# An FFT filter and an MLP on one core: the transform's steps are given out ahead of the inverse's step in the loop over products

## The chip, the core and the metric

The kernel runs on one core of one Trainium2 chip. The metric is the device time of one execution in microseconds (us). A core has five engines that work side by side, each through its own list of instructions in order: TensorE (PE, matrix products, with its weight loads shown as PEld), VectorE (DVE), ScalarE (ACT), GpSimd (POOL) and SyncE (SP), which here does nothing but issue transfers between the device memory and the core. An instruction waits until the data that it reads is there and the buffer that it writes is free.

## What is computed

The reference, cut to what matters. Input x has 8 batches of 3136 positions by 256 channels.

```python
X = np.fft.rfft(x, axis=1)
Y = X * (filt_r + 1j * filt_i)
x = np.fft.irfft(Y, n=3136, axis=1)          # the filtered sequence

X = np.fft.fft(np.fft.fft(x, axis=1), axis=2)
u = x + np.real(X)
un = (u - mean(u)) / np.sqrt(var(u) + 1e-06) # over the channels
out = u + np.maximum(un @ w_ch1, 0.0) @ w_ch2   # 256 -> 1024 -> 256
```

## The kernel before

The two transforms along the sequence cancel in part, so one pass forward and one inverse pass do the work, each as two stages of small matrix products.

*Transform of a batch b* (`there`, 63 steps, `STEPS`). Seven loads bring the batch (`x_b_0` to `x_b_6`, 512 KB each, issued by SP at L399). The largest value of each load is taken, on DVE by a reduction (`mx_b`, L283) or, for batches 1 and 2, on ACT by squares (`xsq_b`, L405). From these a scale is made, which one small product on PE spreads over the partitions (`pb_x`, L276). Fourteen first-stage products follow (`s1_b_0` to `s1_b_13`, L429 for batches 1 and 2, L443 for the others); ACT and DVE write each out (`ast`, L431 and L432) and SP stores it in device memory (`d1<-ast`, L433 or L447). SP reads it back in another order (`at_b_0` to `at_b_6`, L468); the second stage multiplies it (`s<-at`, L493 and L494), the filter is applied on DVE and POOL, a transposing transfer gives `z_b_0` to `z_b_6` (L528), and the inverse's first stage multiplies these (`i<-z`, L563 to L565). Its results are stored (`d2<-bt`, L572).

*Second inverse stage of a batch* (`back`, 17 steps, `BACK`). SP loads `b2_b_0` to `b2_b_6` (L606), PE multiplies (`y_b_0` to `y_b_13`, L629), ACT writes out (`ys`, L639), SP stores (`dy<-ys`, L612).

*Groups of 512 positions* (49 of them, about six to a batch). Group g is fetched from `dy` (`y_g`, L700) and `prepare` makes its input in small pieces: two sets of products on PE (`mix_g`, L713), additions on DVE (L723), the statistics (L782, L783) and the factor `sb_g` (L789 to L798), the normalised value on ACT (`un`, L805), its high and low 16-bit parts on ACT and POOL (`u16`, L808 and L810), and two transposing transfers on SP (`ut_g`, L819).

*Products.* Each group has eight: `h_g_0` to `h_g_7` (L843, six matmuls each), which ACT and DVE turn into `h16` (L852, L853), and for each the part of the second matrix that it feeds (`acc_g_0` and `acc_g_1`, L872, twelve matmuls), two products later (`LAG`). DVE adds the finished `acc` to `y_g` (L881), and SP stores it (`out<-y`, L884).

*The order of the work.* The loop at L1062 goes over all 394 products. In each turn it gives out the first product, a piece of `prepare` of a later group, the second product of two turns before, then at most one step of the inverse's second stage (`give`, L1074), then as many steps of the transform as its progress asks for (`advance`, L1075). `give` stops while the transform of its batch has not been given out to its last but one step (L991); `advance` stops at the start of a batch while the batch before the last has not had its inverse begun (L982). Both only hand work to a scheduler, which keeps its own account of when each engine would be free and ready, and which prefers what was given out earlier where several instructions could go. So the order in which the steps are given out is a rank, and the list of each engine can differ from it. Buffers come from pools with few places (four banks of results for the transform and the small products, two for `h`, two for `acc`, seven places that `x`, `at` and `z` share).

Of the kernel before, what the change touches and what calls it, by code (L numbers as in the profile page):

```python
# [38 lines left out]
STEPS = FIRST + PAUSE + 7 * 5  # L39
WAIT = 2  # L40
BACK = 1 + WAIT + 14
EARLY = 0.6
RISE = 28
# [150 lines left out]
def program(tc, a, NB):  # L194
    nc = tc.nc
    with ExitStack() as ctx:
        _program(ctx, tc, nc, a, NB)


def _program(ctx, tc, nc, a, NB):  # L200
# [491 lines left out]
    def fetch(g):  # L692
        y = ys_of[g] = mp.tile([128, 2, 2, 256], F32, tag="y", name=f"y_{g}", bufs=4)
        for t, (g0, g1) in enumerate(groups[g]):
            q = g0
            while q < g1:
                b = q // NS
                e = min(g1, (b + 1) * NS)
                with after(("un", 0)) if g == 2 else after(("out", g - 4)):
                    marks["y", g] = nc.sync.dma_start(  # L700
                        y[q - g0 : e - g0, t], dys[b][:, q - b * NS : e - b * NS].rearrange("k s c -> s k c")
                    ).ins
                q = e
# [125 lines left out]
    def first_product(g, f):  # L829
        y, ut = ready[g]  # L830
        m = groups[g][0][1] - groups[g][0][0]
        nt = 2 * sum(g1 - g0 for g0, g1 in groups[g])
        utv = ut[:, : len(groups[g])].rearrange("p t (k d l) q -> p t k d l q", k=2, d=2)
        p = ps_h.tile([128, 512], F32, tag="psh", name=f"h_{g}_{f}")
        even = nt == 2 * m * len(groups[g])
        runs = [(slice(0, len(groups[g])), 0, nt, m)] if even else [
            (slice(t, t + 1), 256 * t, 2 * (g1 - g0), g1 - g0) for t, (g0, g1) in enumerate(groups[g])
        ]
        for ts, c0, n, m in runs:
            i = 0  # L840
            for d in range(2):
                for hw, hx in ((0, 0), (0, 1), (1, 0)):
                    marks["pe"] = nc.tensor.matmul(  # L843
                        p[:, c0 : c0 + n].rearrange("p (t k q) -> p t k q", k=2, q=m),
                        w1s[:, d, hw, 128 * f : 128 * f + 128],
                        utv[:, ts, :, d, hx, :m],
                        start=i == 0,
                        stop=i == 5,
                    ).ins
                    i += 1  # L850
        h = mp.tile([128, 2, 512], F16, tag="h", name=f"h16_{g}_{f}", bufs=4)
        marks["relu"] = nc.scalar.activation(h[:, 0, :nt], p[:, :nt], AF.Relu).ins  # L852
        marks["h"] = nc.vector.scalar_tensor_tensor(  # L853
            h[:, 1, :nt], p[:, :nt], 0.0, h[:, 0, :nt], op0=ALU.max, op1=ALU.subtract
        ).ins
        hs[g, f] = h

    def second_product(g, f):
        tiles = groups[g]
        y = ready[g][0]  # L860
        h = hs.pop((g, f))
        if f == 0:
            accs[g] = [
                ps_o.tile([128, 2, 256], F32, tag="pso", name=f"acc_{g}_{t}") for t in range(len(tiles))
            ]
        c0 = 0
        for t, (g0, g1) in enumerate(tiles):
            m = g1 - g0
            acc = accs[g][t]
            for k in range(2):  # L870
                for i, (hh, hw) in enumerate(((0, 0), (0, 1), (1, 0))):
                    nc.tensor.matmul(  # L872
                        acc[:m, k],
                        h[:, hh, c0 : c0 + m],
                        w2s[:, f, hw],
                        start=f == 0 and k == 0 and i == 0,
                        stop=f == 7 and k == 1 and i == 2,
                    )
                c0 += m
            if f == 7:  # L880
                nc.vector.scalar_tensor_tensor(  # L881
                    y[:m, t], acc[:m], beta[:m], y[:m, t], op0=ALU.mult, op1=ALU.add
                )
                marks["sp"] = marks["out", g] = nc.sync.dma_start(a["out"][:, g0:g1].rearrange("k s c -> s k c"), y[:m, t]).ins  # L884
# [93 lines left out]
    def advance(n):  # L978

        while done[0] < min(n, NB * STEPS):  # L980
            b, s = divmod(done[0], STEPS)
            if s == 0 and come[0] < BACK * (b - 1) + 1:  # L982
                return
            if s in folds and b * NS + folds[s] - RING > mixed[0]:
                return
            next(forth)
            done[0] += 1

    def give(n):

        while come[0] < min(n, NB * BACK) and done[0] >= STEPS * (come[0] // BACK + 1) - 1:  # L991
            next(home)
            come[0] += 1
# [3 lines left out]
    def need(slot):  # L997

        return BACK * (slot // NS) + 1 + WAIT + 2 + 2 * (slot % NS // 224)

    def soon(slot):

        return max(need(slot), BACK * ((slot + LOADED) // NS) + 1 + WAIT)

    def bring(slot):
        advance(STEPS * (slot // NS + 1) - 1)
        give(need(slot))
        assert come[0] >= need(slot)
# [52 lines left out]
    per = NS // 32  # L1061
    for q in range(8 * ng + LAG):  # L1062
        g, f = divmod(q, 8)
        if g < ng:
            first_product(g, f)
        if f == 8 - AHEAD:
            for _ in work:
                pass
            if g + 2 < ng:
                work = prepare(g + 2)  # L1070
        next(work, None)
        if q >= LAG:
            second_product(*divmod(q - LAG, 8))
        give(min(come[0] + 1, soon(32 * q + SOON)))  # L1074
        advance(int(STEPS * (1 + min((q + 1) / RISE, (q + 1) / per + EARLY))))  # L1075
        for ahead in [2] * (q == 0) + [g + 3] * (f == 6):
            if ahead < ng:
                bring(groups[ahead][-1][1] - 1)
                fetch(ahead)
# [59 lines left out]
```

## Time and profile before

| | |
|---|---|
| time, median of 3 runs | 1475.76 us (1474.89 to 1478.65) |
| the profiled execution, its own time | 1477.43 us |
| its span, first to last instruction | 1475.5 us |
| PE busy | 1421.5 us, 96% of the span |
| DVE, ACT, POOL busy | 72%, 52%, 36% |
| mean granted TensorE clock | 0.992 of full speed |
| moved by transfers | 280.55 MB, 190 GB/s over the span |

The profile gives, for one execution, the busy time of each engine, the idle time ahead of each instruction with the event that ended it, and the clock that TensorE was granted. Levels of that clock are 2.4 GHz (1.00) and 1.2 GHz (0.50). Idle time of an engine is dear only where what is late next hangs on it.

### The profile page before, as it was taken

What the parts mean: (1) busy time and instruction counts of PE and PEld (TensorE: products, weight loads), DVE (VectorE), ACT (ScalarE), POOL (GpSimd) and SP (SyncE); (2) the same over time, 40 slices, a digit from 0 to 9 for tenths busy, and PEclk for the clock granted to TensorE, in tenths of its full rate; (3) what the DMA queues carried; (4) which work ended last, traced back from release to release, by engine and by line L of the source; (5) the groups of instructions that cost most, each with busy time, mean ns of one, the idle gap of its engine ahead of it and who ended that gap; (6) DMA issues with size and microseconds to landing.
All of it is one profiled execution on the core that took longest, in us unless ns stands there. A gap on an engine that the chain in (4) does not pass through costs nothing.

```text
span 1475.5 us, 30603 instructions
## 1 busy us (share of the span) xinstructions
PE 1421.5 (96%) x11517; PEld 937.5 (64%) x11517; DVE 1069.5 (72%) x2341; ACT 767.4 (52%) x1420; POOL 532.6 (36%) x674
## 2 busy tenths in 40 slices
PE   7897999989999999999999999999999999999998
PEld 3644577546666676667766667666766667666666
DVE  6887677378878876977768876887868786545552
ACT  4766455555556454555447464565446555344341
POOL 4840186028510771038401672028400574010110
PEclk9999999999999999999999999999999999999999
DMA  9956778789976988589775987679684997553320
GB/s 334 325 171 181 199 174 172 251 216 235 226 206 167 203 203 238 148 218 232 164 241 165 234 192 208 183 204 246 153 242 126 220 217 161 142 139 96 86 58 29
DMA packets 445331, 280.55 MB, mean 190 GB/s; under 512 B 218944, under 2 KB 410752, under 8 KB 445184
## 3 DMA queue, kind: packets, MB, share of 16 engines
q1 hardware_dynamic: 445184, 278.61, 72.6%
q8 instruction: 90, 1.47, 0.4%
q14 instruction: 57, 0.47, 0.1%
HBM read 124.88 MB, written 102.79 MB: 154 GB/s over the span
## 4 chain that ended last, share of the span: by engine, by line
PE 67%; DMA 12%; DVE 7%; issue 4%; POOL 4%; ACT 3%; SPq 2%; DVEq 0%; ACTq 0%; POOLq 0%
PE h L843 26%; PE acc L872 25%; PE s L443 3%; DMA x<-x 3%; PE y L629 3%; PE mix L713 2%; DMA at<-d 2%; DMA z<-y 2%; PE s L429 1%; DVE y L723 1%; PE i L563 1%; PE s L493 1%; PE i L565 1%; PE i L564 1%; PE s L494 1%
## 5 line engine op out<-in xcount | busy, mean ns | idle before, releaser
L872 PE MATMUL acc<-w2s,h 128*128 128x256 f16 x4704 | 596.8, 273 | 4.4 <-DVE y L881 2.3
L843 PE MATMUL h<-ut,w1s 128*128 128x512 f16 x2352 | 586.1, 382 | 11.0 <-DVE h L853 4.8
L872 PEld LDWEIGHTS <-h 128*128 128x128 f16 x4704 | 455.9, 98 | 154.8 <-issue 21.5
L852 ACT ACTIVATE h<-h 128x512 f16<-128x512 f32 x392 | 233.1, 595 | 388.1 <-PE h L843 381.2
L853 DVE SCALAR_TENSOR_TENSOR h<-h,h 128x512 f16<-128x512 f32 x392 | 267.9, 685 | 212.5 <-ACT h L852 211.3
L843 PEld LDWEIGHTS <-w1s 128*128 128x128 f16 x2352 | 222.4, 98 | 223.6 <-issue 31.4
L810 POOL TENSOR_TENSOR u<-un,u 128x512 f16<-128x512 f32 x94 | 107.8, 1163 | 678.6 <-ACT u L808 636.7
L723 DVE SCALAR_TENSOR_TENSOR y<-mix,alpha,y 128x508 f32<-128x508 f32 (+1 forms) x368 | 156.1, 476 | 6.7 <-PE mix L713 3.8
L511 POOL TENSOR_TENSOR yt<-yt,t 128x224 f32<-128x224 f32 x112 | 76.5, 683 | 142.2 <-DVE t L507 72.5
L805 ACT ACTIVATE un<-y,sb 128x256 f32<-128x256 f32 x196 | 101.9, 590 | 38.0 <-DVE sb L798 33.9
L517 POOL TENSOR_TENSOR y<-yt,y 128x448 f16<-128x448 f32 x105 | 108.0, 1032 | 18.1 <-ACT y L516 17.9
L571 DVE TENSOR_TENSOR bt<-i,bt 112x512 f16<-112x512 f32 x112 | 76.0, 685 | 48.5 <-ACT bt L570 44.9
L639 ACT ACTIVATE ys<-y,alpha 128x512 f32<-128x512 f32 x112 | 75.9, 685 | 60.6 <-PE y L629 59.1
L570 ACT CAST bt<-i 112x512 f16<-112x512 f32 x112 | 64.5, 584 | 56.9 <-PE i L565 51.7
L881 DVE SCALAR_TENSOR_TENSOR y<-acc,beta,y 128x512 f32<-128x512 f32 x98 | 71.2, 744 | 30.8 <-PE acc L872 30.6
L503 DVE SCALAR_TENSOR_TENSOR yt<-s,pF,ft 128x448 f32<-128x448 f32 x112 | 75.4, 675 | 23.1 <-PE s L494 18.3
L516 ACT CAST y<-yt 128x448 f16<-128x448 f32 x112 | 62.8, 564 | 36.9 <-POOL yt L512 33.0
L556 POOL TENSOR_TENSOR eo<-ef,eo 128x448 f16<-128x448 f32 (+6 forms) x62 | 60.8, 983 | 44.2 <-ACT eo L555 42.7
L507 DVE SCALAR_TENSOR_TENSOR t<-s,pF,ft 128x448 f32<-128x448 f32 x112 | 75.6, 675 | 0.4 <-POOL yt L512 0.3
L535 POOL TENSOR_TENSOR ef<-yt 128x224 f32<-128x224 f32 x112 | 74.1, 679 | 1.6
L512 POOL TENSOR_TENSOR yt<-yt,t 128x224 f32<-128x224 f32 x112 | 73.7, 660 | 0.0
L629 PE MATMUL y<-b,i 112*64 112x512 f16 (+1 forms) x480 | 70.2, 375 | 3.0 <-DMA b<-d 1.3
(131 smaller groups left out, 1656.7 us busy)
## 6 DMA issues: line engine op xcount, KB each, us to landing
x<-x SPq DMA_DIRECT2D x56, 512.0 KB
at<-d SPq DMA_DIRECT2D x56, 512.0 KB
b<-d SPq DMA_DIRECT2D x56, 512.0 KB
d<-ast SPq DMA_DIRECT2D x112, 224.0 KB
d<-bt SPq DMA_DIRECT2D x112, 224.0 KB
out<-y SPq DMA_DIRECT2D x98, 256.0 KB
y<-dy SPq DMA_DIRECT2D x92, 256.0 KB
dy<-ys SPq DMA_DIRECT2D x208, 112.0 KB
```

What stands on the lines that cost most here:

```text
L511: nc.gpsimd.tensor_tensor(yh[:, 0], yh[:, 0], t2v[:, 1], op=ALU.subtract)
L517: last = half(b, hf == 1).tensor_tensor(ylo, ytv, yhi, op=ALU.subtract)
L571: marks["low"] = nc.vector.tensor_tensor(bt[:, :, 1], p, bt[:, :, 0], op=ALU.subtract).ins
L629: marks["i2"] = nc.tensor.matmul(p[64 * h : 64 * h + 64, js], i2[:, t, h, i], bt[:, o + js.start : o + js.stop, h], start=i == 0, stop=i == 1,
L639: nc.scalar.activation(ys[:, o : o + 2], p, AF.Copy, scale=al[:, 2:3])
L723: nc.vector.scalar_tensor_tensor(out, p, al, y, op0=ALU.mult, op1=ALU.add)
L805: nc.scalar.activation(un[:m, k], y[:m, t, k], AF.Identity, bias=sb[:m, i, 1:2], scale=sb[:m, i, 3:4])
L810: marks["u16", g] = low.tensor_tensor(u16[:m, :, :, 1], unv, u16[:m, :, :, 0], op=ALU.subtract).ins
L843: marks["pe"] = nc.tensor.matmul(p[:, c0 : c0 + n].rearrange("p (t k q) -> p t k q", k=2, q=m), w1s[:, d, hw, 128 * f : 128 * f + 128], ut ...
L852: marks["relu"] = nc.scalar.activation(h[:, 0, :nt], p[:, :nt], AF.Relu).ins
L853: marks["h"] = nc.vector.scalar_tensor_tensor(h[:, 1, :nt], p[:, :nt], 0.0, h[:, 0, :nt], op0=ALU.max, op1=ALU.subtract).ins
L872: nc.tensor.matmul(acc[:m, k], h[:, hh, c0 : c0 + m], w2s[:, f, hw], start=f == 0 and k == 0 and i == 0, stop=f == 7 and k == 1 and i == 2,)
```

## The change

Two lines of the loop over products change places. What each step does is the same, and no instruction is added or left out.

```diff
         if q >= LAG:
             second_product(*divmod(q - LAG, 8))
+        advance(int(STEPS * (1 + min((q + 1) / RISE, (q + 1) / per + EARLY))))
         give(min(come[0] + 1, soon(32 * q + SOON)))
-        advance(int(STEPS * (1 + min((q + 1) / RISE, (q + 1) / per + EARLY))))
```

Within a turn the transform's steps now rank ahead of the inverse's step. Each transform step stays in its turn. The first inverse step of batches 1 to 6, which had to wait for the transform steps of the turn before, is given out one turn earlier (batch 1 in turn 27 instead of 28). The scheduler makes other lists from this: 8891 of PE's 22910 rows, 795 of DVE's 2343, 549 of ACT's 1396, 215 of POOL's 679 and 406 of SP's 1070 stand at another place; what lies ahead of the loop is the same but for one small product (`y_0_10`, now inside the loop), and from about 1260 us on the lists are the same again.

**Place one, between batches 1 and 2 (around 260 to 317 us).** SP's list before, from the last but one load of batch 2 on; `dy_1`, `b2_1` belong to batch 1's second inverse stage, `out<-y_3` and `y_6` to groups (the trailing numbers are the program's own):

```order
L399 DMA x_2_5_3269<-x 128x1024
L606 DMA b2_1_1_3346<-d2_1_128 128x8x256
L884 DMA out<-y_3_1936 128x2x256
L612 DMA dy_1_3261<-ys_1_0_3348 28x256 x2
L612 DMA dy_1_3261<-ys_1_0_3348 28x4x256
L612 DMA dy_1_3261<-ys_1_0_3348 28x3x256
L612 DMA dy_1_3261<-ys_1_0_3348 28x4x256
L612 DMA dy_1_3261<-ys_1_0_3348 28x3x256
L606 DMA b2_1_2_3404<-d2_1_128 128x8x256
L399 DMA x_2_6_3270<-x 128x1024
```

and now:

```order
L399 DMA x_2_5_3269<-x 128x1024
L606 DMA b2_1_1_3346<-d2_1_128 128x8x256
L399 DMA x_2_6_3270<-x 128x1024
L884 DMA out<-y_3_1936 128x2x256
L612 DMA dy_1_3231<-ys_1_0_3348 28x256 x2
```

The last load of batch 2, `x_2_6`, has moved ahead of an output store, six stores and a load. DVE's list at the same place before, where `y_6` is group 6's additions, `ast_2` the write-out of batch 2's first stage and `h16_5` the products of group 5:

```order
L432 SCALAR_TENSOR_TENSOR ast_2_1_3516<-s1_2_1_3514,sx_2_3461,ast_2_1_3516 112x2x256
L853 SCALAR_TENSOR_TENSOR h16_5_4_4046<-h_5_4_4039,h16_5_4_4046 128x512
L432 SCALAR_TENSOR_TENSOR ast_2_2_3522<-s1_2_2_3520,sx_2_3461,ast_2_2_3522 112x2x256
L853 SCALAR_TENSOR_TENSOR h16_5_5_4101<-h_5_5_4094,h16_5_5_4101 128x512
L723 SCALAR_TENSOR_TENSOR y_6_3371<-mix_6_3536,al_6_0_3650,y_6_3371 128x4x127
```

and now:

```order
L432 SCALAR_TENSOR_TENSOR ast_2_1_3507<-s1_2_1_3505,sx_2_3451,ast_2_1_3507 112x2x256
L432 SCALAR_TENSOR_TENSOR ast_2_2_3513<-s1_2_2_3511,sx_2_3451,ast_2_2_3513 112x2x256
L723 SCALAR_TENSOR_TENSOR y_6_3371<-mix_6_3536,al_6_0_3650,y_6_3371 128x4x127
L723 SCALAR_TENSOR_TENSOR y_6_3371<-mix_6_3536,al_6_0_3650,y_6_3371 128x2x127 x2
L723 SCALAR_TENSOR_TENSOR y_6_3371<-mix_6_3536,al_6_0_3650,y_6_3371 128x4
L723 SCALAR_TENSOR_TENSOR y_6_3371<-mix_6_3536,alpha_1_2157,y_6_3371 128x4x127
L853 SCALAR_TENSOR_TENSOR h16_5_3_3987<-h_5_3_3980,h16_5_3_3987 128x512
```

Group 6's additions have moved ahead of group 5's `h16_5_3`, `h16_5_4` and `h16_5_5`. On PE the two sets of `mix_6` stand earlier by so many matmuls that lie between; worked out from the lengths of these, the first by 5.65 us of products and the second by 6.9 us, while `h_5_3` to `h_5_7` and the last `acc_5` stand later.

**Place two, between batches 6 and 7 (around 1095 us).** SP's list before:

```order
L399 DMA x_7_4_15077<-x 128x1024
L399 DMA x_7_5_15078<-x 128x1024
L606 DMA b2_6_2_15237<-d2_0_126 128x8x256
L399 DMA x_7_6_15079<-x 128x1024
L700 DMA y_36_15249<-dy_6_15005 64x2x256
```

and now:

```order
L399 DMA x_7_4_15077<-x 128x1024
L399 DMA x_7_5_15078<-x 128x1024
L399 DMA x_7_6_15079<-x 128x1024
L606 DMA b2_6_2_15240<-d2_0_126 128x8x256
L700 DMA y_36_15249<-dy_6_14976 64x2x256
```

The load `x_7_6` and the load `b2_6_2` have changed places.

**Place three, between batches 4 and 5 (around 754 to 768 us).** DVE's list before, where `mx_5` are the reductions over batch 5's loads and `h16_21` the products of group 21:

```order
L283 TENSOR_REDUCE mx_5_10337<-x_5_0_10330 112x1
L853 SCALAR_TENSOR_TENSOR h16_21_4_10384<-h_21_4_10377,h16_21_4_10384 128x512
L723 SCALAR_TENSOR_TENSOR y_23_10177<-mix_23_10287,alpha_3_6234,y_23_10177 128x4x127
L283 TENSOR_REDUCE mx_5_10337<-x_5_1_10331 112x1
L723 SCALAR_TENSOR_TENSOR y_23_10177<-mix_23_10287,alpha_3_6234,y_23_10177 128x2x127 x2
```

and now:

```order
L283 TENSOR_REDUCE mx_5_10337<-x_5_0_10330 112x1
L283 TENSOR_REDUCE mx_5_10337<-x_5_1_10331 112x1
L853 SCALAR_TENSOR_TENSOR h16_21_4_10384<-h_21_4_10377,h16_21_4_10384 128x512
L723 SCALAR_TENSOR_TENSOR y_23_10177<-mix_23_10299,alpha_3_6225,y_23_10177 128x4x127
L283 TENSOR_REDUCE mx_5_10337<-x_5_2_10332 112x1
```

One reduction has moved ahead of `h16_21_4`, and in the rows that follow one more each ahead of `h16_21_5`, `h16_21_6` and `h16_21_7`.

## Rows read from the trace of the kernel before

**Rows 1.** The page's table of engines: busy time, share of the span, instructions.

```profile
PE 1421.5 (96%) x11517; PEld 937.5 (64%) x11517; DVE 1069.5 (72%) x2341; ACT 767.4 (52%) x1420; POOL 532.6 (36%) x674
```

**Rows 2.** Stretches of 60 us: length, then the busy time of PE, PEld, DVE, ACT and POOL with their instructions, the granted clock, the busy share of the transfer engines, GB/s; the last row is the sum over 24 such stretches.

```profile
0.00:60.00 60.00, 51.63 (x432) 28.32 (x433) 43.81 (x82) 31.81 (x55) 35.44 (x54) 1.00 0.97 339
60.00:120.00 60.00, 51.38 (x376) 28.34 (x375) 50.03 (x101) 40.48 (x73) 27.84 (x31) 0.97 0.71 225
...
300.00:360.00 60.00, 55.05 (x500) 34.52 (x498) 47.20 (x109) 32.30 (x62) 35.42 (x48) 0.94 0.93 215
360.00:420.00 60.00, 57.87 (x481) 39.36 (x478) 46.15 (x88) 30.89 (x60) 27.41 (x34) 1.00 0.92 232
...
1260.00:1320.00 60.00, 60.00 (x440) 38.37 (x438) 32.59 (x89) 26.38 (x50) 6.67 (x6) 1.00 0.50 122
...
sum 1440.00, PE 1390.41 PEld 916.09 DVE 1059.14 ACT 760.82 POOL 532.61; mean PE 57.93 PEld 38.17 DVE 44.13 ACT 31.70 POOL 22.19
```

**Rows 3.** What PE waited for over the whole span: in total, times, longest, in us.

```profile
PE s L493 <- DMA at<-d: 10.5, 8, 3.0
PE pb_w L276 <- DVE lines_w L274: 5.2, 2, 4.8
PE h L843 <- DVE h L853: 4.8, 6, 1.4
PE i L563 <- DMA z<-y: 4.7, 5, 1.8
PE h L843 <- DMA dy<-ys: 4.7, 1, 4.7
...
PE acc L872 <- DVE y L881: 2.3, 1, 2.3
```

**Rows 4.** PE's instructions in order of time, from several short stretches: start, length, what; in brackets the idle time just before and what ended it.

```profile
181.59 0.20 PE L493 MATMUL s<-s,at 112*128 112x56 f16 x1 [1.87 <-DMA at<-d]
...
205.90 0.29 PE L563 MATMUL i<-z,i 112*112 112x256 f16 x1 [1.57 <-DMA z<-y]
...
379.86 1.47 PE L843 MATMUL h<-ut,w1s 128*128 128x512 f16 x6 [1.44 <-DMA ut<-u]
...
765.07 1.46 PE L843 MATMUL h<-ut,w1s 128*128 128x512 f16 x6 [1.35 <-DVE h L853]
...
985.76 0.20 PE L493 MATMUL s<-s,at 112*128 112x56 f16 x1 [2.14 <-DMA at<-d]
...
1106.88 1.14 PE L872 MATMUL acc<-w2s,h 128*128 128x256 f16 x8 [2.34 <-DVE y L881]
```

**Rows 5.** PE in order of time between batches 1 and 2, with the same columns: the product that waits for the scale, the two sets of `mix_6` and the first products of group 6.

```profile
276.39 1.46 PE L843 MATMUL h<-ut,w1s 128*128 128x512 f16 x6
...
281.49 0.21 PE L276 MATMUL pb_x<-lines_x,still 112*128 112x112 bf16 x1
...
289.41 0.56 PE L713 MATMUL mix<-mix,eo 128*128 128x129 f16 x8
...
291.89 0.56 PE L713 MATMUL mix<-mix,eo 128*128 128x129 f16 x8
...
317.02 3.57 PE L843 MATMUL h<-ut,w1s 128*128 128x512 f16 x8 [4.65 <-DMA dy<-ys]
```

**Rows 6.** SP's issues between batches 1 and 2, in order of time: an output store, a load of the inverse, the last load of batch 2, and the second transposing transfer of group 6.

```profile
260.76 5.67 SPq L884 DMA_DIRECT2D out<-y  x1
...
271.97 0.38 SPq L399 DMA_DIRECT2D x<-x  x1
...
312.47 1.70 SPq L819 DMA_TRANSPOSE ut<-u  x1
```

**Rows 7.** The chain of waits at the same place (start, length, what): the load `x_2_5`.

```profile
259.52 10.21 DMA x<-x
```

**Rows 8.** ACT in order of time at the same place: the square of the last load, `x_2_6`.

```profile
277.05 1.06 ACT L405 ACTIVATE xsq<-x 112x1024 bf16<-112x1024 f32 x1 [2.44 <-DMA x<-x]
```

**Rows 9.** Short stretches, with the columns of rows 2: two of heavy transfer at place one, the stretch of the low clock there, and the same at place two.

```profile
255.00:265.00 10.00, 10.00 (x74) 6.34 (x72) 1.93 (x6) 4.02 (x8) 0.00 (x0) 1.00 0.99 314
265.00:275.00 10.00, 8.55 (x59) 4.96 (x58) 2.77 (x4) 8.30 (x16) 0.00 (x0) 1.00 0.90 299
...
1100.00:1105.00 5.00, 4.14 (x25) 2.25 (x24) 2.07 (x5) 1.14 (x3) 0.00 (x0) 1.00 1.08 317
...
315.80:322.60 6.80, 5.58 (x15) 2.13 (x16) 3.07 (x15) 1.05 (x3) 0.00 (x0) 0.50 0.97 272
1107.70:1111.10 3.40, 3.40 (x12) 1.46 (x11) 1.63 (x6) 1.65 (x4) 0.00 (x0) 0.50 0.45 154
```

**Rows 10.** DVE in order of time at place two: the last two reductions over batch 7's loads, with the idle time before each.

```profile
1101.09 1.22 DVE L283 TENSOR_REDUCE mx<-x 112x1 f32<-112x1024 f32 x1 [1.39 <-DMA x<-x]
...
1104.88 1.22 DVE L283 TENSOR_REDUCE mx<-x 112x1 f32<-112x1024 f32 x1 [1.85 <-DMA x<-x]
```

**Rows 11.** SP's issues at place two: the two loads that change places.

```profile
1095.37 0.38 SPq L606 DMA_DIRECT2D b<-d  x1
1095.79 1.14 SPq L399 DMA_DIRECT2D x<-x  x1
```

**Rows 12.** DVE in order of time at place three: the first reduction over batch 5's loads and what follows it.

```profile
753.72 1.22 DVE L283 TENSOR_REDUCE mx<-x 112x1 f32<-112x1024 f32 x1 [2.47 <-DMA x<-x]
754.86 0.68 DVE L853 SCALAR_TENSOR_TENSOR h<-h,h 128x512 f16<-128x512 f32 x1
```

## The prediction

> **What bounds the kernel now.** I read the page's table of engines first. PE is busy for 1421.5 of 1475.5 us [rows 1], so the kernel is bound by PE's products, and since the change adds and drops none, the only time that it can win or lose is PE's idle time and the time that PE spends at the low clock. The stretches of 60 us say where idle time is: PE is busy 1390.4 of the first 1440 us, and 17.0 of the missing 49.6 us lie in the first 120 us (8.4 and 8.6), which the change leaves as they are. From 1260 us on PE is never idle [rows 2]. So some 32.6 us between 120 and 1260 us are all the idle time there is to win.
>
> The list of PE's waits says what ended it: reads of the transform's stage 1 (10.5 us in 8 waits), `h16` from DVE (4.8 in 6), `z` (4.7 in 5), one wait of 4.7 us at the first product of a group, one of 2.3 for an addition on DVE, and one of 4.8 at the scale of the weights ahead of the loop [rows 3]. All but the last are places where an instruction of the transform, the inverse or a group's preparation came late for PE's next row, and such places depend on the order in the lists. The two largest are in PE's own rows: 4.65 us ahead of the first product of group 6 (317.02) and 2.34 us ahead of group 34's second product (1106.88) [rows 4, 5]. The clock adds to both: from 315.8 to 322.6 and from 1107.7 to 1111.1 us the granted clock was 0.50, that is 1.2 GHz, after PE had stood idle, and PE was busy 5.58 and 3.40 us of these [rows 9]. At 2.4 GHz this work takes half, so the low clock cost 2.8 and 1.7 us.
>
> **The change, part by part.** No instruction comes or goes, so every edit is a move, and I price what each does to these waits.
>
> *Place one, group 6.* The wait named as `dy<-ys` at 317.02 is really for `ut_6`, whose second transposing transfer SP issued at 312.47 and was done issuing at 314.17 [rows 6]. Ahead of it lies the chain mix, additions, statistics, normalised value, `u16`. Before, the two sets of `mix_6` ran at 289.41 and 291.89 [rows 5]. By the order they now stand 5.65 and 6.9 us of products earlier, and DVE's list has the additions ahead of three `h16_5` rows. From the second set to the wait's end is a chain that needs no other late work, so `ut_6` comes about 6 us earlier and 4.65 are needed: the wait goes, and the low clock with it, -4.65 and -2.8. What is late next is the scale of batch 2. `pb_x` now stands where PE comes at about 276.6 (behind the product that starts at 276.39), and it ran at 281.49, 4.4 us after the square of `x_2_6` began at 277.05, which had waited for the load [rows 5, 8]. That load was issued at 271.97, held behind an output store that kept SP for 5.67 us from 260.76 [rows 6]. It now goes ahead of that store, so 11 us sooner, but into full transfer engines (busy 0.99 and 0.90) [rows 9]. The load ahead of it landed at 269.73 (259.52 + 10.21) [rows 7]. Two loads of 512 KB at 314 GB/s [rows 9], 3.3 us, bring `x_2_6` to 273.1 and `pb_x` to 277.5: a new wait of +0.9. Bounds: 0 if it lands at 272, +4.9 if it lands no sooner than before. I take +0.9, from the rates. Place one: -6.55.
>
> *Place two, batch 7's last load.* DVE works through its list in order: the reduction at 1104.88 had waited 1.85 us for `x_7_6`, the addition that frees PE's bank stood behind it, and PE waited 2.34 us [rows 4, 10]. SP now issues `x_7_6` ahead of `b2_6_2` instead of after it (1095.37 and 1095.79 [rows 11]). The reduction over the load before, which also waited, began at 1101.09, so the two landed 3.79 us apart with `b2_6_2` between them: 1.05 MB in that time is 277 GB/s, close to the 317 of that stretch [rows 9, 10]. So these transfers were served about in the order of issue, and the swap is worth half of the 3.79, 1.9, plus the issue slot of 0.4. I take -2.0 of the 2.34, and the low clock goes, -1.7. Bounds: 0 and -4.0. Place two: -3.7. The Trainium skill (DMA: Bandwidth & Descriptors, "Queues, rings and completion order") says that each transfer engine takes one issuer's descriptors in ring order, with which these rows agree, but also that a later transfer may complete before an earlier one. If the two loads simply shared the engines, the swap would give the issue slot alone, 0.4 us, the low clock would stay, and the sum would come out 3.3 us higher.
>
> *Place three, DVE at batch 5.* Four reductions move ahead of `h16_21_4` to `h16_21_7`. The next instruction starts 1.14 us after a reduction does (753.72 to 754.86) [rows 12]. PE already waits 1.35 us at 765.07 for an `h16` there [rows 4], so at least one of them is on the path: +1.1. Bounds: 0 and four times that, +4.6.
>
> *The small places* [rows 4], the shifts on PE worked out like those of `mix_6` from the products that lie between. At 181.59 the reads of stage 1 get two store issues of some 0.4 us (as in [rows 11]) in front of them: +0.7. At 205.90 the transposing transfers of `z_1_1` pass one of a group on SP; one holds SP for up to 1.70 us [rows 6], more than the 1.57 that PE waited: -1.6. At 379.86 the first product of group 8 stands 1.4 us later on PE with `ut_8` about where it was; 0 to -1.44, I take half, -0.7. At 985.76 the second stage's first product stands 3 us later, which covers its 2.14, but `z_6_0` falls behind a transposing transfer of group 31 and an output, which gives back 1.4: -0.7. With place three this is -1.2. The rest (gaps under 2 us at batches 1 to 6, and `y_0_10`, now inside the full loop) I put at -1.5, between -4 and +2.
>
> *Waits that the trace of before can't show.* 8891 rows of PE's list stand elsewhere. The waits of before in [rows 3], without that for the weights, come to 27.0 us in 21, 1.3 us each. I expect some five new ones of that size, +6.4. Bounds: 0, and ten of them, +13.
>
> *Sum.* -6.55 - 3.7 - 1.2 - 1.5 + 6.4 = -6.55. Against the profiled execution's own 1477.43 us this is 1470.9; that execution lay 1.67 above the median of 1475.76, so the median should come to 1469.2. I forecast **1469 us**. What tells a difference from none is about 0.3%, 4.4 us.
>
> **Rivals.**
>
> *The waits are handed on.* PE runs ahead by what place one frees and meets the transfers of the next groups: the transfer engines are busy 0.93 and 0.92 of the time from 300 to 420 us [rows 2], and 1.08 at place two [rows 9]. Group 8, which waited 1.44 at 379.86 [rows 4], would then wait the 6.55 longer, and after place two the next load or fetch likewise. For it: transfers don't get faster by an order. Against it: in the stretch that bounds `ut_6` nothing but PE's order was late, and what prepares group 8 on PE moves forward with PE. Only the small places are left then, -1.2 - 1.5, and the handed-on waits are the new ones: 1475.76 - 2.7 = 1473.1, no change that can be told.
>
> *Everything that can go goes.* No new wait of weight: without the +6.4 the sum is -13, 1462.8. For it: DVE, ACT and POOL have room [rows 1]. Against it: as many rows moved back as forward.
>
> *Slower: instructions that need a load now stand ahead of ready work.* At place one the square of `x_2_6` on ACT and `pb_x` on PE, at place three the reductions on DVE, and each engine stops until the load is there. If `x_2_6` lands no sooner than before, `pb_x` costs 4.9 instead of 0.9 (+4.0), PE falls to 1.2 GHz after so long a wait as it did at 317.02 (+2.8), all four reductions count (4.6 instead of 1.1, +3.5), and `x_7_6` comes no sooner either (+3.7): -6.55 + 14.0 = +7.4, 1483.2. It decides from where `x_2_6` lands after 275 us. For it: 0.99 and 0.90 in those stretches [rows 9], 10.21 us for the load before [rows 7]. Against it: that load stood behind five of the same batch, and `x_2_6` now follows it with only one 512 KB load between. The Trainium skill (TensorE: Matmul & The Clock Gate, "Architectural detail") calls ScalarE and VectorE strictly in order, and the reduction at 1104.88 that held PE for 2.34 us shows it here.
>
> That the change does nothing, since steps only give a rank, is excluded by the lists, which differ.
>
> **How the numbers follow.** The forecast's own case gets 0.46, everything goes 0.10, handed on 0.25, slower 0.19. So faster by over 0.3% has 0.56, within it 0.25, slower 0.19. The forecast's own range is 1464 to 1471. The range for 8 in 10 reaches from beyond the case in which all goes (1460, with the far bounds of places one and two) to short of the full slower case (1481).
>
> **What would show it.** Right: no wait over 1 us ahead of group 6's first product, `pb_x` of batch 2 with a wait of about 1 us, a granted clock of 1.00 around 310 to 325 and 1105 to 1115 us, DVE's last reduction of batch 7 waiting under 0.5 us, and in the list of PE's waits about 25 us from 120 to 1260 us instead of 32.6. Wrong: the wait at group 6 found again at group 7 or 8 (handed on); `pb_x` of batch 2 waiting 4 us or more, or waits for `h16` doubled to 10 us (slower); or a new low-clock stretch at another batch's start, which I haven't priced singly.

## The result, and the profile after

The changed kernel took 1494.76 us (median of 3 runs, 1488.33 to 1495.60) against 1475.76 before: a ratio of 1.0102, with a 95% interval from 1.0077 to 1.0126. It is slower, by 1%, and lies outside the range that was forecast. Two later comparisons, on two chips, gave 1.0087 (1.0063 to 1.0111) and 1.0104 (1.0084 to 1.0124).

The page of the changed kernel, table of engines, answers to [rows 1]; its span is 1493.8 us:

```profile
PE 1434.2 (96%) x11517; PEld 945.0 (63%) x11517; DVE 1070.4 (72%) x2341; ACT 766.2 (51%) x1420; POOL 534.0 (36%) x674
```

The same number of instructions kept PE busy 12.7 us longer. From the first product of group 0 to the end (columns of [rows 2]) the kernel before shows

```profile
123.50:1475.50 1352.00, 1318.53 (x10710) 880.87 (x10709) 972.14 (x2147) 693.46 (x1289) 469.34 (x590) 0.99 0.72 181
```

and the changed one

```profile
123.30:1493.80 1370.50, 1329.07 (x10714) 886.69 (x10713) 974.10 (x2146) 692.93 (x1290) 470.76 (x590) 0.99 0.71 179
```

This stretch is 18.5 us longer: PE is idle 41.4 us instead of 33.5, 7.9 more, and busy 10.5 more with the same products. A part of the longer work is work at the low clock. These are the stretches of the changed kernel at the low clock behind 200 us, with the same columns; before there were two, of 6.8 and 3.4 us [rows 9]:

```profile
227.10:230.50 3.40, 3.40 (x19) 1.60 (x15) 2.81 (x5) 3.40 (x8) 3.40 (x6) 0.50 1.12 132
322.70:326.10 3.40, 3.40 (x20) 1.71 (x16) 2.65 (x7) 0.00 (x0) 2.21 (x4) 0.50 0.92 278
408.00:411.40 3.40, 3.40 (x16) 1.55 (x13) 2.31 (x7) 2.28 (x7) 0.00 (x0) 0.50 1.08 345
674.30:677.70 3.40, 3.40 (x25) 2.25 (x24) 0.69 (x1) 1.27 (x2) 2.19 (x3) 0.50 1.22 195
834.70:841.50 6.80, 6.29 (x61) 3.96 (x57) 4.46 (x9) 0.60 (x1) 5.37 (x8) 0.50 0.76 176
1275.00:1278.40 3.40, 3.40 (x11) 0.96 (x10) 1.11 (x5) 0.69 (x1) 0.00 (x0) 0.50 0.38 96
```

PE was busy 23.3 us in these, against 9.0 in the two of before; half of the difference, 7.2 us, is lost to the clock. (The other 3.3 of the 10.5 I can't assign.) This execution has the lowest mean clock, 0.984, of all 15 runs of the changed kernel; how much of the loss goes with the clock over all of them stands below.

The waits of PE over the whole span, as [rows 3]:

```profile
PE s L493 <- DMA at<-d: 13.6, 13, 3.0
PE i L563 <- DMA z<-y: 7.8, 8, 2.2
PE y L629 <- DMA b<-d: 5.8, 4, 2.9
PE h L843 <- DVE h L853: 5.1, 5, 1.5
```

The single wait of 4.7 for `ut_6` and the one of 2.3 for an addition are gone from the list. In their place stand more and smaller waits for reads (13 instead of 8), for `z` (8 instead of 5), and four of 5.8 us in all for the loads `b2` of the inverse, which before had 0.3 us behind 123 us. PE in order of time, with the idle time in brackets, shows where (as [rows 4]):

```profile
319.80 0.20 PE L493 MATMUL s<-s,at 112*128 112x56 f16 x1 [0.91 <-DMA at<-d]
322.33 0.20 PE L493 MATMUL s<-s,at 112*128 112x56 f16 x1 [1.52 <-DMA at<-d]
...
346.95 1.25 PE L843 MATMUL h<-ut,w1s 128*128 128x512 f16 x5 [1.30 <-DMA ut<-u]
...
406.66 0.60 PE L629 MATMUL y<-b,i 112*64 112x256 f16 x7 [2.87 <-DMA b<-d]
...
673.74 0.32 PE L563 MATMUL i<-z,i 112*112 112x256 f16 x1 [2.07 <-DMA z<-y]
...
771.54 1.46 PE L843 MATMUL h<-ut,w1s 128*128 128x512 f16 x6 [1.46 <-DVE h L853]
...
775.95 1.46 PE L843 MATMUL h<-ut,w1s 128*128 128x512 f16 x6 [1.64 <-DMA b<-d]
...
834.07 0.20 PE L493 MATMUL s<-s,at 112*128 112x56 f16 x1 [2.18 <-DMA at<-d]
835.79 0.23 PE L493 MATMUL s<-s,at 112*128 112x56 f16 x1 [0.51 <-DMA at<-d]
...
1118.05 1.46 PE L843 MATMUL h<-ut,w1s 128*128 128x512 f16 x6 [1.33 <-DVE h L853]
...
1193.62 0.32 PE L563 MATMUL i<-z,i 112*112 112x256 f16 x1 [2.16 <-DMA z<-y]
...
1273.46 0.63 PE L629 MATMUL y<-b,i 112*64 112x256 f16 x8 [2.15 <-DMA b<-d]
```

Behind the waits at 322, 406, 673, 834 and 1273 lies a low-clock stretch of the table above each time. Ahead of the one at 227 PE waited four times, 0.4 to 0.6 us each, and behind the 2.16 us at 1193.62 there is none. Group by group: the first product of group 6 starts 4.7 us sooner than before, that of group 7 2.0 us later, group 8 3.5, group 9 7.0, group 14 5.7, group 19 9.0, group 24 16.5, group 35 13.2, group 40 and all after 18.3.

### The profile page after: what moved, and what is told of

Its sections match the earlier page's. It is cut to its first block, busy times and chain, and to the rows that moved or that the text cites. A ratio compares the mean times of both kernels' runs of the same rounds, so it can differ in the third digit from the quotient of the medians.

```text
span 1493.8 us, 30582 instructions
## 1 busy us (share of the span) xinstructions
PE 1434.2 (96%) x11517; PEld 945.0 (63%) x11517; DVE 1070.4 (72%) x2341; ACT 766.2 (51%) x1420; POOL 534.0 (36%) x674
## 4 chain that ended last, share of the span: by engine, by line
PE 63%; DMA 12%; DVE 9%; issue 5%; ACT 4%; POOL 3%; SPq 2%; DVEq 0%; ACTq 0%; POOLq 0%
PE h L843 25%; PE acc L872 24%; DMA x<-x 3%; PE y L629 3%; PE s L443 2%; PE mix L713 2%; DMA at<-d 2%; DMA d<-ast 2%; DVE y L723 2%; DVE h L853 1%; DMA z<-y 1%; PE i L563 1%; DMA b<-d 1%; PE i L564 1%; PE i L565 1%
## 5 line engine op out<-in xcount | busy, mean ns | idle before, releaser
L511 POOL TENSOR_TENSOR yt<-yt,t 128x224 f32<-128x224 f32 x112 | 76.6, 684 | 152.6 <-DVE t L507 127.4
L493 PE MATMUL s<-s,at 112*128 112x56 f16 x896 | 62.9, 190 | 15.0 <-DMA at<-d 13.6
```

Of the source, the lines that this page charges most:

```text
L511: nc.gpsimd.tensor_tensor(yh[:, 0], yh[:, 0], t2v[:, 1], op=ALU.subtract)
```

## The experiments

One thing in the section on the change has to be set right first. The change does not only alter the rank within a turn. The inverse's steps 0 to 4 of batches 1 to 7 are given out one turn earlier, because the last transform step that they wait for now comes ahead of them in the turn. (At batch 1 these are steps 0 to 2 alone.) Steps 0 to 2 do little but the load; step 3 has the first product `y_b_0`. I had written of the first step alone and of batches 1 to 6. So there are two edits, the rank and the earlier turn. All runs below compare with runs of the kernel before on the same chip (medians 1475.4 to 1476.8 us).

| run | what it is | us | ratio to before, 95% |
|---|---|---|---|
| e1_rank | rank alone | 1476.4 | 1.0005 (0.9987 to 1.0023) |
| e2_gate | earlier turn alone | 1483.3 | 1.0048 (1.0028 to 1.0067) |
| e3_early | change, turns 0 to 111 | 1479.8 | 1.0025 (1.0007 to 1.0042) |
| e4_late | change, from turn 112 | 1481.5 | 1.0029 (1.0015 to 1.0043) |
| e5_after_again | the change | 1490.8 | 1.0087 (1.0063 to 1.0111) |
| e7_pin | `y_b_0` one product sooner | 1478.9 | 1.0014 (1.0001 to 1.0027) |
| e8_turn1 | earlier turn, batch 1 | 1476.0 | 1.0001 (0.9986 to 1.0017) |
| e9_turn2 | earlier turn, batch 2 | 1476.9 | 1.0004 (0.9990 to 1.0017) |
| e10_turn4 | earlier turn, batch 4 | 1477.5 | 1.0000 (0.9983 to 1.0018) |
| e11_later | first product a turn later | 1475.8 | 0.9994 (0.9980 to 1.0009) |
| e12_rank_turn14 | rank, earlier turn at 1 to 4 | 1485.7 | 1.0064 (1.0039 to 1.0089) |
| e13_rank_turn57 | rank, earlier turn at 5 to 7 | 1479.8 | 1.0030 (1.0013 to 1.0047) |
| e14_turn57 | earlier turn at 5 to 7 | 1479.8 | 1.0027 (1.0013 to 1.0041) |
| e15_rank_late | rank from turn 200 | 1471.8 | 0.9966 (0.9951 to 0.9981) |
| e16_without4 | change, batch 4's turn as before | 1483.1 | 1.0040 (1.0025 to 1.0056) |
| e17_without2 | change, batch 2's turn as before | 1490.2 | 1.0093 (1.0072 to 1.0113) |
| e18_after_third | the change | 1492.5 | 1.0104 (1.0084 to 1.0124) |

**The two edits apart.** The rank alone:

```diff
+        was = done[0]
+        advance(int(STEPS * (1 + min((q + 1) / RISE, (q + 1) / per + EARLY))))
-        give(min(come[0] + 1, soon(32 * q + SOON)))
+        give(min(come[0] + 1, soon(32 * q + SOON)), was)
-        advance(int(STEPS * (1 + min((q + 1) / RISE, (q + 1) / per + EARLY))))
```

where `give` looks at `was` instead of `done[0]`. (By the condition at L982 the first two transform steps of batch 2 then come a turn later, which the change itself doesn't do.)

> The transform's steps rank ahead of the inverse's within a turn, as in the change, but the inverse's first step waits for what the turns before gave out, as before the change, so no inverse step comes a turn earlier. Theory A (the earlier turn of the inverse's first steps, whose products then stand on PE ahead of their loads, is the cost): about the time before, 1472 to 1480 us, and no wait for b2 over 1 us. Theory B (the rank inside a turn is the cost): about the time of the change, 1488 to 1496. Theory C (every departure from the order before costs some waits, wherever it comes from): in between, 1480 to 1490.

The earlier turn alone:

```diff
+        upto = min(come[0] + 1, soon(32 * q + SOON))
-        give(min(come[0] + 1, soon(32 * q + SOON)))
+        give(upto)
         advance(int(STEPS * (1 + min((q + 1) / RISE, (q + 1) / per + EARLY))))
+        give(upto)
```

> The inverse's step stays ahead of the transform's steps within a turn, but where it was held back for its batch's transform it is given out at the end of the same turn, one turn earlier than before. Theory A: about the change's time, 1488 to 1496, with waits for b2 at batches 2 and 7 of 2 to 3 us. Theory B: 1472 to 1480. Theory C: 1480 to 1490.

The rank alone moved 8083 rows of PE's list and cost nothing that can be told; the earlier turn moved 4468 and cost 7 us. So theory B falls, and moved rows are no measure of a loss. Theory A isn't met either: it wanted 1488 to 1496 us of the earlier turn alone, and 1483.3 lies in the range of theory C. In the profiles PE is idle 33.7 us behind its first product with the rank alone and 39.5 with the earlier turn alone, against 33.5 before. Waits of PE in the rank alone, from 123 us on:

```profile
PE s L493 <- DMA at<-d: 12.2, 12, 1.7
PE i L563 <- DMA z<-y: 5.8, 6, 1.8
...
PE y L629 <- DMA b<-d: 0.6, 1, 0.6
```

and in the earlier turn alone:

```profile
PE h L843 <- DVE h L853: 9.6, 11, 1.9
...
PE y L629 <- DMA b<-d: 4.0, 4, 1.8
```

The rank brings the waits for reads and `z`, the earlier turn those for `h16` and for `b2`. (Before, from 123 us on, the reads have 7.3 us, `z` 4.7, the `h16` 4.8 and `b2` 0.3.) The change has both, and costs more than the 7.9 us of the two together.

**By place.** `advance` ahead of `give` for `q < 112` or for `q >= 112` alone.

> The change in the first 112 turns only (products of groups 0 to 13, to about 500 us), the order before from there on. If the lost time sits in places that do not depend on one another, the product of group 14 starts 5.7 us later than before, as in the change, and the whole is 5.7 us longer: about 1481. If what is lost there is made up later (or draws more behind it), the whole differs from that by over 4.

> The change from turn 112 on only. Independent places: 18.3 - 5.7 = 12.6 us longer than before, about 1488, with the load x_7_6 of batch 7 still in time (the 2.3 us wait at the second product of group 34 gone). Otherwise differs from that by over 4.

They gave +0.25% and +0.29%; their sum, 0.54%, is less than the change's 0.87 to 1.04, and the late half cost 0.29% where 0.85 was expected. That was no proof against independent places, because a single profile, from which the 5.7 and 12.6 us had come, is not the median. So both kernels were taken again.

> The changed kernel once more, beside more runs of the kernel before. If the low clock is the larger part of the loss, its runs spread over several us and the fast ones show a mean clock near 0.992, some 1488 us, the slow ones 0.985 and 1495. If the loss is idle time alone, the runs stay within 3 us of 1494.8 whatever the clock. If the two edits add up (rank +0.5, earlier turn +7.4 us), the median is near 1484.

> The kernel before once more, for a second profile. Waits that the order sets stand again at the same instructions within 0.5 us: 4.65 at the first product of group 6, 2.34 at the second product of group 34, 2.1 at batch 6's first read. A wait that an accident of the transfers made in the first profile is gone or halved; I expect that of the 2.34 at group 34, since the run with the change in the first 112 turns alone, whose lists there are those of before, had only about 1 us.

The kernel before, once more, one run of 1473.5 us: the wait at group 6 is there (4.42), the one at group 34 has halved, and no low-clock stretch follows it:

```profile
1104.72 0.49 PE L872 MATMUL acc<-w2s,h 128*128 128x256 f16 x3 [1.20 <-DVE y L881]
```

The changed kernel's runs spread over 12.5 us and follow the clock: 1483.7 us at a mean clock of 0.994, 1496.2 at 0.985. Over its 15 runs a mean clock lower by 0.001 goes with 1.13 us more (correlation -0.89); for 127 runs of the kernel before it is 0.60 us (-0.55). At 0.992 the change took 1487 to 1490 us in four runs, so 11 to 14 us are lost even there. And the kernels hardly differ in their clock: it is 0.9889 in the mean of the 15 runs and 0.9902 in that of the 127. At 1.13 us for 0.001 this is 1.5 us of the 15.5 by which the mean times differ. The clock explains the spread of the changed kernel's runs; most of its loss it does not.

The profiles say the same, now that there are three of the changed kernel (the third is e18's) and two of the kernel before. Idle and busy time of PE are counted from about the first product of group 0 to the end, the low clock behind 200 us:

| profile | its time, us | mean clock | PE idle, us | PE busy, us | of it at the low clock |
|---|---|---|---|---|---|
| before | 1477.4 | 0.992 | 33.5 | 1318.5 | 9.0 |
| before, e6 | 1473.5 | 0.992 | 32.3 | 1316.1 | 3.4 |
| change | 1495.6 | 0.984 | 41.4 | 1329.1 | 23.3 |
| change, e5 | 1496.2 | 0.985 | 45.2 | 1325.6 | 16.2 |
| change, e18 | 1497.6 | 0.988 | 46.5 | 1324.7 | 9.9 |

The third profile of the change has about as much work at the low clock as the first of before, and is the longest of the five.

**The first product ahead of its load.** In the kernel, `y_b_0` is held behind the product of its turn. Here it is held behind the one before, and nothing else is moved:

```diff
+        if "pe" in marks:
+            marks["pe0"] = marks["pe"]
         if g < ng:
             first_product(g, f)
...
-            with after("pe") if c == 0 and b else after("warm") if b == 0 and c < 8 else nullcontext():
+            with after("pe0") if c == 0 and b else after("warm") if b == 0 and c < 8 else nullcontext():
```

> The kernel before, but the first product of each inverse (y_b_0) may start one product of the loop earlier; its step stays in its turn. Theory A1 (the earlier turn costs because y_b_0 comes ahead of its load): y_2_0 stands ahead of the last product of group 8 and waits 2 to 3 us for b2_2_0, and the time is 3 to 5 us longer, 1479 to 1481. Theory A2 (it costs through all the steps that come a turn earlier, whose stores, loads and results crowd the queues): within 1.5 us of before.

+2.0 us, between the two theories, and the wait that was to explain it (`y_2_0` for its load) was 0.46 us in its profile. So I moved the turn at single batches (the second `give(upto)` only where `come[0] // BACK` is 1, 2 or 4), and the other way round.

> The kernel before, with the inverse's first steps one turn earlier at batch 1 alone. In the run with the earlier turn at all batches the first product of group 8 started 2.6 us earlier than before. Theory A2 (steps that come earlier cost wherever they come): slower by 1 us or more. Theory D (each batch has its own price, some below nothing, and only the sum is a loss): 1 to 3 us faster than before.

> The same at batch 2 alone. Theory A1 (y_2_0 ahead of its load): slower by 2 to 3.5 us, with a wait of about 2 us for b2_2_0, as when only its place was loosened (+2.0). Theory A2: slower by clearly more than that. Theory D: 2 to 3.5 us.

> The same at batch 4 alone. Here no product comes ahead of a load, but the reductions over batch 5's loads come ahead of four h16 on DVE. Place three as predicted: waits for h16 around group 21 grow from 1.5 to 2.6 us or more, slower by 1.1 to 4.6 us, nearer 2.5. If DVE has room there: within 1 us of before.

> The kernel before, with the inverse's first product step one turn later at every batch, the other way round. If earlier costs because products and reductions come ahead of what they need, later gives nothing or a little: -2 to +1 us. Theory C (the order before is one that fits, and every departure loses): slower by 3 us or more.

All four lie at the time before, so none of the theories A1, A2 and D is met at batches 1 and 2 where it gives a number. (Batch 3 alone was not run.) `y_2_0` waited 0.35 us with the turn at batch 2 alone, where it waits 2.87 in the change. At batch 4 the waits for `h16` did grow, to 2.75 us from 1.35 [rows 4], within what the time can tell:

```profile
765.28 1.46 PE L843 MATMUL h<-ut,w1s 128*128 128x512 f16 x6 [1.11 <-DVE h L853]
769.69 1.46 PE L843 MATMUL h<-ut,w1s 128*128 128x512 f16 x6 [1.64 <-DVE h L853]
```

Theory C falls with e11: another order is not dearer as such.

**Which batches.** Rank everywhere, with the earlier turn at some batches only (`was if come[0] // BACK >= 5 else None`, and the reverse); the turn at batches 5 to 7 alone; the rank from turn 200 on alone.

> The change with the earlier turn kept only at batches 1 to 4; at batches 5 to 7 only the rank is changed. Theory E (the two edits clash late: what the rank gains at batches 5 to 7, about 9 us in its profile, is lost when the inverse's first steps also come a turn earlier there): 1481 to 1485, clearly faster than the change. Theory F (they clash at batches 1 to 4, where the first products of the inverse wait behind full transfer engines): within 2 us of the change, 1489 to 1491.

> The change with the earlier turn kept only at batches 5 to 7. Theory E: 1485 to 1489, most of the loss. Theory F: 1476 to 1480.

> The kernel before with the earlier turn at batches 5 to 7 alone, the rank as before. If each batch has its own price, the 7 us of the earlier turn at all batches that batches 1, 2 and 4 did not show lie here: 1481 to 1484. If the price comes only when many batches are moved, within 2 us of before.

> The rank alone, from turn 200 (group 25) on. In the profile of the rank alone the groups from 25 on ran 9 us faster than before, 2 to 3 of which are a wait that differs between the two profiles of before. If places are independent, 1469 to 1472, faster than the kernel before. If it was a draw of one execution, 1475 to 1478.

At batches 5 to 7 the earlier turn costs 0.27% alone and 0.25% beside the rank: about the same 4 us, so no clash of the two edits can be told there, and e13, in the range of theory F, misses that of E. The 1485.7 us of e12 lie between the two ranges. At batches 1 to 4 the turn costs 0.59% beside the rank (1.0064 against 1.0005). e15 is faster than the kernel before, 1471.8 against 1475.4 us. Its profile, from the first product of group 0 on, shows PE idle 29.7 us and busy 1314.8 (before 33.5 and 32.3, 1318.5 and 1316.1):

```profile
124.40:1468.80 1344.40, 1314.75 (x10710) 881.31 (x10709) 970.79 (x2146) 691.75 (x1289) 470.04 (x590) 1.00 0.72 183
```

Between 830 and 1270 us its waits of PE come to 2.9 us; in the two profiles of before they are 7.5 and 6.8.

**Two waits taken away from the change.** The rank everywhere, the earlier turn everywhere but at batch 4 (`was if come[0] // BACK == 4 else None`), or but at batch 2.

> The change, but with the inverse's first steps of batch 4 in their old turn; all else as in the change. If the reductions ahead of four h16 at place three are a part of the loss beside the changed rank: the waits for h16 around group 21 and 22 (3.5 to 3.8 us in three profiles) fall under 2 us, and the time is 2 to 5 us under the changed kernel of the same call. If not: within 1.5 us of it.

> The change, but with the inverse's first steps of batch 2 in their old turn. If y_2_0 ahead of its load counts: the wait of 2.8 to 3.0 us for b2_2_0 near 405 us is gone, and the time is 2 to 4 us under the changed kernel of the same call. If a later wait takes it back: within 1.5 us of it.

> The changed kernel, to compare these two with on the same chip: 1488 to 1492 us, and among its runs again 1 to 1.2 us more for each 0.001 less of mean clock.

Without batch 4's turn 9.4 us of the 16.3 are gone (1483.1 against 1492.5; from the two intervals some 4 either way). Without batch 2's it is 2.3, which the intervals don't tell from nothing, though its wait went from 2.87 to 0.40. In the traces of e16 and of the change every engine runs the same instructions in the same order but for a stretch from 751 to 882 us, so the 9.4 us come from what differs there. PE's waits between 740 and 860 us in the change:

```profile
PE s L493 <- DMA at<-d: 2.7, 2, 2.2
PE h L843 <- DMA b<-d: 1.6, 1, 1.6
PE h L843 <- DVE h L853: 1.5, 1, 1.5
PE i L563 <- DMA z<-y: 0.5, 1, 0.5
```

and without batch 4's turn:

```profile
PE s L493 <- DMA at<-d: 0.3, 1, 0.3
PE h L843 <- DVE h L853: 0.2, 1, 0.2
```

DVE in order of time shows where the waits for `h16` come from. In the change the reductions over batch 5's loads (L283) stand one by one ahead of `h16_21_4` to `h16_21_7`, and PE's rows at 771.54 and 775.95 start 0.74 and 0.73 us after an `h16` does, when it is written:

```profile
762.54 1.22 DVE L283 TENSOR_REDUCE mx<-x 112x1 f32<-112x1024 f32 x1 [2.32 <-DMA x<-x]
764.60 1.22 DVE L283 TENSOR_REDUCE mx<-x 112x1 f32<-112x1024 f32 x1 [0.84 <-DMA x<-x]
...
769.68 1.21 DVE L283 TENSOR_REDUCE mx<-x 112x1 f32<-112x1024 f32 x1
770.80 0.68 DVE L853 SCALAR_TENSOR_TENSOR h<-h,h 128x512 f16<-128x512 f32 x1
771.40 1.21 DVE L283 TENSOR_REDUCE mx<-x 112x1 f32<-112x1024 f32 x1
...
774.09 1.21 DVE L283 TENSOR_REDUCE mx<-x 112x1 f32<-112x1024 f32 x1
775.22 0.68 DVE L853 SCALAR_TENSOR_TENSOR h<-h,h 128x512 f16<-128x512 f32 x1
```

(The second of these two waits is named after a load; the `h16` at 775.22 ended it.) Without batch 4's turn the loads are there sooner: the first reduction starts 8.2 us behind the first product of group 21 (744.85), where in the change it is 14.3 us (748.25), and five of the seven are done before the `h16` at 764.15:

```profile
753.08 2.33 DVE L283 TENSOR_REDUCE mx<-x 112x1 f32<-112x1024 f32 x2
...
756.74 1.21 DVE L283 TENSOR_REDUCE mx<-x 112x1 f32<-112x1024 f32 x1
...
760.34 2.33 DVE L283 TENSOR_REDUCE mx<-x 112x1 f32<-112x1024 f32 x2
...
764.15 0.68 DVE L853 SCALAR_TENSOR_TENSOR h<-h,h 128x512 f16<-128x512 f32 x1
766.11 1.22 DVE L283 TENSOR_REDUCE mx<-x 112x1 f32<-112x1024 f32 x1 [1.28 <-DMA x<-x]
```

With the rank alone it is 8.2 us too, in the kernel before 14.4 and with the turn at batch 4 alone 14.7. So the rank brings these loads 6 us forward, and batch 4's earlier turn takes that back. The waits for `h16` are some 3 of the 9.4 us: 3.1, 3.5 and 3.2 us in the three profiles of the change, 0.2 without batch 4's turn. With the turn at batch 4 alone they are 2.75, and that cost nothing against the 1.35 of before. The rest of the 9.4 lies further on. Against the kernel before (mean of its two profiles), in us:

| | group 21 to 23 | group 23 to 25 |
|---|---|---|
| the change, three profiles | +1.3, +1.7, +1.3 | +7.0, +2.7, +5.1 |
| the change without batch 4's turn | -1.8 | +0.7 |
| the rank alone | -2.2 | +2.3 |
| the turn at batch 4 alone | +1.5 | -0.5 |

## Why the prediction was wrong

The forecast is a sum of idle time, 2.05 us less in the end, and of the clock, 4.5 us less. The step that failed is the idle time: against the mean of the two profiles of before, PE was idle 8.5, 12.2 and 13.6 us longer in the three of the change. By what PE waited for, from 123 us on and again in means: the waits that shrank (for `ut` and for the addition on DVE) gave 4.6 us, where the sum has 11.2 of gains; those that grew took 14.8, where it has 9.1 of new waits with the +6.4 among them. The 14.8 are `b2` 5.4, `z` 3.6, reads 3.2 and `h16` 2.6 us. The term that was to hold such waits was five times an average of before, without a row that said where; and the largest of them, the waits for `b2`, comes with the earlier turn (4.0 us with it alone, 0.6 with the rank alone), which the prediction doesn't price.

*The change itself* was read as a rank, with an earlier turn of one step. The turn is what costs: 7 us by itself at all batches, 4 us at batches 5 to 7 with the rank or without, 9.4 at batch 4 beside the rank. What is left for batches 1 to 3 and the rank (16.3 - 4 - 9.4, some 3 us) can't be told from nothing.

*Place one* was right in its main term: the wait of 4.65 is gone in all three profiles. The load `x_2_6` was not as early as worked out. Its issue held SP for 5.85 us, its square, which waited for it, starts at 275.78, where the landing was expected at 273.1, and `pb_x` runs at 279.80 instead of 277.5:

```profile
263.65 5.85 SPq L399 DMA_DIRECT2D x<-x  x1
...
275.78 1.06 ACT L405 ACTIVATE xsq<-x 112x1024 bf16<-112x1024 f32 x1 [1.24 <-DMA x<-x]
```

Yet `pb_x` had no wait of note, since PE came to it later than I had it. What failed is the sentence that `pb_x` is what is late next. Late next were `at_2_0` and `at_2_1` (0.91 and 1.52), a low clock at 322.7, and `ut_7` (1.30), and group 8 started 3.5 us later than before. That is the rival that hands the waits on, seen at this place.

*Place two* was an accident of one execution. The second profile of the kernel before shows 1.20 us for the wait of 2.34 and no low clock, so there 1.2 of the -3.7 was to be won at most. From group 34 to group 35 that profile is 3.4 us shorter than the first, and those of the change are 3.0, 4.1 and 4.0 shorter: beside the second profile less than 1 us is won.

*Place three* was about right in the wait that it priced and wrong in what follows. I took +1.1, with a bound of +4.6, and the waits for `h16` there grew by some 1.7 to 2.1 us. The reads and the `z` behind them, 1.8 to 3.2 us in the three profiles, and the low clock behind these (3.1, 0 and 1.5 us) were not in the sum. The rival that forecast "slower" had the direction, but not for its reasons: `pb_x` cost nothing instead of 4.9, and the four reductions not their 4.6.

*The clock* was to give 4.5 us back. In the first profile it cost 7.2 more than before instead; in the third it cost 0.5 more, with the largest loss of the three. Over all runs it goes with some 1.5 us. The prediction says that a low-clock stretch at another batch's start was not priced singly; it should have been a term, but by all runs it is the smaller part of the loss.

What stays open: why the turn at batch 4 costs 9.4 us beside the changed rank and 0 (between -0.17 and +0.18%) without it. A part can be read from the rows: beside the rank the turn undoes the 6 us by which the rank brings the loads of batch 5 forward, and without it there is nothing to undo. The larger part arises between groups 23 and 25, where reads of batch 5 and the low clock add waits in the change; but reads wait 1.7 us there with the rank alone, too. No run took these apart. Also open is which of the shorter waits behind 830 us makes the gain of e15: the 0.34% is the interval's, the places are those of single profiles.

## What to carry to other kernels

Where a change moves when steps are given out, find first which steps come a whole turn earlier, and what each of them stands in front of in an engine that works in order; the number of moved rows says nothing about it. Read a wait as a gain only when a second profile shows it again. Before a loss is put down to the clock, compare the mean clocks of all runs of both kernels, not one profile of each. And expect the end of one wait to be in part handed on to the next load or fetch. An edit that loses as a whole can hold a part that wins: the rank in the last part of the loop alone made this kernel 0.34% faster.

## What the runs showed that was not expected

The low clock made this kernel, with its many short waits, not only slower but uneven, and a single profile then misleads. The changed kernel's runs lie between 1483.67 and 1497.63 us, and the same order gave low-clock stretches at other places in each profile: behind 200 us at 227, 323, 408, 674, 835 and 1275 us in the first, at 227, 661, 678 and 1275 in the second, at 409, 840 and 1276 in the third. Ahead of five of the six in the first stood a wait of 1.5 to 2.9 us, while one of 2.14 [rows 4] in the kernel before and one of 2.16 in the change passed without a stretch. What stayed the same in all three profiles are waits: for `b2` near 406 us (2.87, 2.65, 2.70) and 1274 us (2.15, 2.01, 1.93), for `z` near 1194 us (2.16, 2.12, 2.01).
